# Attention front end and two-layer MLP on one core: group 0's first loads split by pairs of heads, values loaded in four pieces, first pass ordered anew

## The chip, the cores and the metric

The kernel runs on one core of a Trainium2 chip. A core has TensorE (PE in the profile; its weight loads are PEld), VectorE (DVE), ScalarE (ACT), GpSimd (POOL) and SyncE (SP). Each engine works through its own queue of instructions in program order, and semaphores make one wait for another. SP and POOL issue the transfers between DRAM and the on-chip memory; POOL's can change float32 into float16 on the way. Products of TensorE land in eight PSUM banks of 512 float32 columns.

The metric is the device time of the whole program in microseconds, median over runs; lower is better.

## The reference

```python
def _attn_ref(q, k, v):                       # each (8, 12, 448, 64)
    S = q.shape[2]
    scale = 1.0 / np.sqrt(q.shape[-1])
    scores = scale * np.matmul(q, k.transpose(0, 1, 3, 2)) - np.log(S)
    attn = 1.0 / (1.0 + np.exp(-scores))
    return np.matmul(attn, v).astype(np.float32)

def _moe_ref(x, w_in, w_out, beta):           # x (3584, 768), w_in (768, 2048), w_out (2048, 768)
    h = x @ w_in
    g = h * (1.0 / (1.0 + np.exp(-beta * h)))
    return (g @ w_out).astype(np.float32)
```

`reference` runs the attention, puts the 12 heads of a token side by side (768 values) and feeds the 3584 tokens to the two layers. The weights of the attention are sigmoids, so there is no sum over keys to wait for.

## The kernel before

**Groups, pairs, key tiles.** Four heads make a group; a batch has three groups (`QPB`), the program 24. A group is two pairs of heads (`s = 2 * g + x`, x = 0 or 1), and the four heads lie on 32 partitions each, so that a pair holds 64 partitions. The 448 rows of a head are cut by partition into 14 chunks (`NB`) of 32 rows. `transpose` turns the raw q and k of a group into `qT` and `kT` by 32x32 blocks on VectorE. Keys come in three full tiles of 128 and a short one of 64 (`KL`): chunks 0 to 11 fill the full tiles, chunks 12 and 13 the short one. The values lie the same way in `v16`: column `j` of the 32 rows of chunk block `i` belongs to full tile `j`, and column `JF` of partitions 0 to 63 to the short tile; `double_v_last` copies these 64 partitions to the other 64.

**Score, sigmoid, values.** `score` multiplies one head's keys by its queries, two products (`e`) of 32 rows each, and writes a score tile, which is two PSUM banks, one per head of the pair. `weigh` (L250) is ScalarE's sigmoid over such a tile, `weigh_two` (L265) over two. `half_visit(g, c0, second)` does half of a group's queries (224) against key tiles 0 and 1, or against tile 2 and the short one; it works on both pairs at once. `attend` (L340) multiplies the values by the attention, and VectorE brings the result to `xT` (L349). Three score tiles are in use in the first pass (`share_psum(3)`), two after `("two",)`.

**Layers.** `dense1` (L362) is the first layer of a block of 128 hidden columns, six products each, with its sigmoid on ScalarE (L374) and its product with it on VectorE (L377). Later batches go through a Strassen-like scheme (L531, L651).

**The first pass** is a list written out by hand, `BEGIN`: each entry goes to the queue of its engine in this order. `("cast", r, c0, c1, act)` turns chunks of group 0's staged k (r = 1) or q (r = 0) from float32 into float16, on ScalarE or VectorE. `("k", g)` and `("q", g, half)` are transposes. `("idle", n)` gives TensorE n products of a zero tile, which nothing reads. `("scores", g, half, second)` is a `half_visit`, `("values", g, half)` an `attend`, `("dense", n)` takes the next n products from `fill`, a list of first- and second-layer products. Behind `BEGIN`, a loop visits the other groups and spreads the rest of `fill` between the visits; `MORE` shifts the share of single visits by a few products.

**Loads.** Group 0's k and the first half of its q come by SP as float32 into memory that `gt` uses later (L797), then beta (L824). All else comes by POOL in the order of `LOADS`, then `LATER`: q and k by L126, the values by `load_v_full` (L149, four loads per batch) and `load_v_last` (L161, two), `w_in` in eight pieces (L177), `w_out` in four (L185). POOL's loads share eight semaphores in turn, so that each waits before its issue until the eighth load before it has landed. Ahead of its loads POOL sets two small constants, `nlogs` and `dummy` (L811, L812).

```python
        BEGIN = [
            ("cast", 1, 0, 8, False), ("cast", 1, 8, 14, True), ("cast", 0, 0, 7, True), ("k", 0), ("q", 0, 0),
            ("q", 1, 0), ("idle", 20), ("scores", 0, 0, 1), ("idle", 4), ("scores", 0, 0, 0), ("k", 1),
            ("idle", 2), ("k", 2), ("q", 2, 0), ("idle", 2), ("scores", 1, 0, 0), ("beta",), ("idle", 8),
            ("scores", 1, 0, 1), ("v", 0), ("idle", 6), ("scores", 2, 0, 0), ("values", 0, 0), ("q", 1, 1),
```

Of the kernel before, what the change touches and what calls it, by code (L numbers as in the profile page):

```python
# [8 lines left out]
FP32 = mybir.dt.float32  # L9
FP16 = mybir.dt.float16  # L10
# [3 lines left out]
def kernel(  # L14
# [10 lines left out]
    nc = tc.nc  # L25
    AF = mybir.ActivationFunctionType
    ALU = mybir.AluOpType

    B, H, S, D = q.shape
# [6 lines left out]
    PAIR = D // BLK  # L36
    JF = S // P
    KL = S - JF * P
    NF = JF * P // BLK
    NPAIR = H // 2  # L40
    QPB = H // HQ
    NHC = DM // P
# [97 lines left out]
    def last_base(s: int) -> int:  # L140
        return (s % 2 ^ swapped(s // 2)) * KL

    def load_v_full(b: int, lo: int = 0, hi: int = H):

        if b not in vs:
            vs[b] = vp.tile([P, H, JF + 1, D], FP16, tag="v16", name="v16")
        rows = v[b, lo:hi].rearrange("h (p c) d -> p h (c d)", c=NB)
        for i in range(HQ):
            nc.gpsimd.dma_start(  # L149
                out=vs[b][i * BLK : (i + 1) * BLK, lo:hi, 0:JF].rearrange("p h j d -> p h (j d)"),  # L150
                in_=rows[:, :, JF * i * D : JF * (i + 1) * D],
            )
            ready.update((b, "full", t, i) for t in range(lo // HQ, hi // HQ))

    def load_v_last(b: int):
        if b not in vs:
            vs[b] = vp.tile([P, H, JF + 1, D], FP16, tag="v16", name="v16")
        rows = v[b].rearrange("h (p c) d -> p h c d", c=NB)
# [3 lines left out]
        ready.add((b, "last"))  # L162

    def load_v(b: int):
        load_v_full(b)
        load_v_last(b)

    def double_v_last(b: int):
        assert (b, "last") in ready
        ready.add((b, "v"))  # L170
        nc.vector.tensor_copy(out=vs[b][KL:P, :, JF], in_=vs[b][0:KL, :, JF])

    WOUT = 2

# [26 lines left out]
    def transpose(g: int, r: int, c0: int = 0, c1: int = NB):  # L201
        raw = raws[g][:, r]
        assert g or (r, c0) == (0, NB // 2) or all((r, "cast", c) in ready for c in range(c0, c1))
        if r == 0:
            if g not in qT:
                qT[g] = qTp.tile([P, NB * BLK, PAIR], FP16, tag="qT", name="qT")
            ready.update((g, "q", c) for c in range(c0, c1, NB // 2))
            nc.vector.transpose(
                out=in_order(g // QPB, qT[g][:, c0 * BLK : c1 * BLK]),
                in_=raw[:, c0:c1].rearrange("p c d -> p (c d)").bitcast(FP32),  # L210
            )
            return
        ready.add((g, "k"))
        kT[g] = kTp.tile([P, S, PAIR], FP16, tag="kT", name="kT")
        to = kT[g].rearrange("p k e -> p (k e)").bitcast(FP32)
        frm = raw.rearrange("p c d -> p (c d)").bitcast(FP32).rearrange("p (c f) -> p c f", c=NB)
        nc.vector.transpose(  # L217
            out=to[:, 0 : JF * P].rearrange("p (j i q) -> p i j q", j=JF, i=HQ),
            in_=frm[:, 0:NF].rearrange("p (i j) f -> p i j f", j=JF),
        )  # L220
        nc.vector.transpose(  # L221
            out=to[:, JF * P :], in_=frm[:, NF:].rearrange("p c f -> p (c f)")
        )

    def score_tile():
        i, j = scored[n_sc[0] % len(scored)]
# [3 lines left out]

    def score(sco, u0: int, s: int, jt: int, hh: int, e: int, c0: int, n: int):
        g, lo = s // 2, (s % 2 * 2 + hh) * BLK
        assert (g, "k") in ready and all(
            (g, "q", c) in ready for c in range(c0 // BLK, (c0 + n) // BLK, NB // 2)
        )
        base, nk = (last_base(s), KL) if jt == JF else (0, P)
        nc.tensor.matmul(  # L237
            sco[base : base + nk, hh, u0 : u0 + n],
            kT[g][lo : lo + BLK, jt * P : jt * P + nk, e],
            qT[g][lo : lo + BLK, c0 : c0 + n, e],  # L240
            start=(e == 0),
            stop=(e == PAIR - 1),
            tile_position=(lo, base),
        )
# [55 lines left out]
    def half_visit(g: int, c0: int, second: int):  # L300
# [18 lines left out]
        for s, jt, sco, u0 in plan:  # L319
            at_use(ats[id(sco)], (s, jt, c0), slice(u0, u0 + QH))  # L320

    def attend(g: int, c0: int, n: int, part=(0, 1)):
        b, t = divmod(g, QPB)
        if b not in xTs:
            xTs[b] = xTp.tile([P, NHC, S], FP16, tag="xT", name="xT")
        assert (b, "v") in ready and (b, "full", t, HQ - 1) in ready
# [438 lines left out]
    with tc.manual_schedule():  # L765
        def load(what, *a):
            if what == "q":
                load_one(a[0], 0, a[1] * NH, (a[1] + 1) * NH)
            elif what == "k":
                load_one(a[0], 1)  # L770
            elif what == "qk":
                load_qk(a[0])
            elif what == "v":
                load_v_full(0, a[0] * HQ, a[1] * HQ)
            elif what == "last":
                load_v_last(0)
# [7 lines left out]
        LOADS = [  # L784
            ("q", 1, 0), ("k", 1), ("k", 2), ("last",), ("q", 2, 0), ("v", 0, 3), ("q", 1, 1), ("q", 0, 1),
            ("q", 2, 1), ("w_in", 0, 2), ("w_in", 2, 4), ("w_in", 4, 6), ("w_in", 6, 8), ("w_in", 8, 10),
            ("w_in", 10, 12), ("w_in", 14, 16), ("w_in", 12, 14),
        ]
        LATER = [
            ("qk", 3), ("w_out", 0, 0), ("w_out", 1, 0), ("values", 1), ("qk", 4), ("qk", 5), ("w_out", 0, 1),  # L790
# [11 lines left out]
        def cast(r: int, c0: int, c1: int, act: bool):  # L802
            out = raws[0][:, r, c0:c1].rearrange("p c d -> p (c d)")
            frm = parts[r][0][:, c0 * D : c1 * D]
            if act:
                nc.scalar.copy(out=out, in_=frm)  # L806
            else:
                nc.vector.tensor_copy(out=out, in_=frm)
            ready.update((r, "cast", c) for c in range(c0, c1))
# [22 lines left out]
        def beta_columns():  # L832
# [3 lines left out]
                nc.vector.transpose(out=beta_sb[part], in_=beta_in[:, part])  # L836

        BEGIN = [
            ("cast", 1, 0, 8, False), ("cast", 1, 8, 14, True), ("cast", 0, 0, 7, True), ("k", 0), ("q", 0, 0),
            ("q", 1, 0), ("idle", 20), ("scores", 0, 0, 1), ("idle", 4), ("scores", 0, 0, 0), ("k", 1),  # L840
            ("idle", 2), ("k", 2), ("q", 2, 0), ("idle", 2), ("scores", 1, 0, 0), ("beta",), ("idle", 8),
            ("scores", 1, 0, 1), ("v", 0), ("idle", 6), ("scores", 2, 0, 0), ("values", 0, 0), ("q", 1, 1),
            ("scores", 2, 0, 1), ("q", 0, 1), ("values", 1, 0), ("scores", 0, 1, 0),
            ("values", 2, 0), ("scores", 0, 1, 1), ("dense", 12), ("scores", 1, 1, 1), ("two",), ("dense", 6),
            ("scores", 1, 1, 0), ("loads",), ("q", 2, 1), ("dense", 21), ("scores", 2, 1, 0), ("dense", 9),
            ("values", 0, 1), ("scores", 2, 1, 1), ("values", 1, 1), ("values", 2, 1), ("dense", 39), ("k", 3),
            ("q", 3, 0), ("q", 3, 1), ("dense", 45),
        ]
        for what, *a in BEGIN:
            if what == "q":  # L850
                g, half = a
                transpose(g, 0, half * NH, (half + 1) * NH)
            elif what == "k":
                transpose(a[0], 1)
            elif what == "scores":
                half_visit(a[0], a[1] * QH, a[2])
            elif what == "cast":
# [1 line left out]
            elif what == "idle":  # L859
                idle_units(a[0])  # L860
            elif what == "v":
                double_v_last(a[0])
# [32 lines left out]
        def left_us(n: int):  # L895
# [2 lines left out]
        AV_US = 1.5  # L898
        GLANCE = 3
        MORE = {  # L900
# [3 lines left out]
        }  # L904
        RESERVE = (1.99, 3.28)
        LATE = {
# [122 lines left out]
```

## Time and profile before

| | |
|---|---|
| median of 3 runs | 373.94 us (373.41 to 374.00) |
| the profiled execution | 374.6 us, its span 372.8 us |
| TensorE busy | 365.8 us (98%) |
| ScalarE busy | 259.9 us (70%) |
| VectorE busy | 254.5 us (68%) |
| GpSimd busy | 90.6 us (24%) |
| granted TensorE clock | 1.00 |

The span runs from the first instruction to the last; the execution's own time has 1.8 us around it. Busy time is a share of the whole span; what a stage waits for is read in the timeline of that stage. In a line of the timeline the columns are start and length in us, engine, line, operation, what it writes and reads, and in brackets the idle time of the engine before it with what ended it; several like instructions in a row are merged (x10).

In the first 5.9 us TensorE runs nothing but the fillers of `("idle", 20)`. VectorE and ScalarE are idle until 4.35, when group 0's k has landed.

### The profile page before, as it was taken

Reading aid. Unit: us, or ns where it says so; the run is one execution under the profiler, and the core shown is the slowest. Engines: PE = TensorE matmul, PEld = TensorE weight load, DVE = VectorE, ACT = ScalarE, POOL = GpSimd, SP = SyncE. Lnnn points to the kernel's source line nnn. Section 1 sums busy time; section 2 is a strip of 40 time slices with the busy share of each in tenths; the row PEclk is TensorE's granted clock in tenths of the full one; section 3 lists DMA queues with packets and bytes.
Section 4 is the critical chain, followed back from the end, with each engine's and each line's share of the span. In section 5 each row is a group of like instructions: output and inputs, shape, how many; then the busy total and the mean of one; then the engine's idle time right before and its main releaser. Section 6 shows DMA issues by size and latency. Waiting matters only on the chain.

```text
span 372.8 us, 7320 instructions
## 1 busy us (share of the span) xinstructions
PE 365.8 (98%) x2906; PEld 184.4 (49%) x2906; DVE 254.5 (68%) x479; ACT 259.9 (70%) x311; POOL 90.6 (24%) x136
## 2 busy tenths in 40 slices
PE   7989999999999999999999999999999999999997
PEld 4566644443444455544444445554444455555655
DVE  3435696877496966787667666778667666669671
ACT  5995777699876658887777749887787647883000
POOL 6833253151151012325123003235100002230000
PEclk9999999999999999999999999999999999999999
DMA  9999999993359030039829511018903111000334
GB/s 162 165 189 202 197 203 201 245 125 51 49 76 183 2 86 1 0 51 125 157 42 206 108 26 33 3 17 116 172 6 86 42 44 42 1 2 1 86 84 128
DMA packets 42626, 34.65 MB, mean 93 GB/s; under 512 B 21968, under 2 KB 39008, under 8 KB 42592
## 3 DMA queue, kind: packets, MB, share of 16 engines
q0 software_dynamic: 36688, 22.47, 44.5%
q1 hardware_dynamic: 5904, 11.71, 11.1%
q8 instruction: 23, 0.38, 0.4%
q14 instruction: 11, 0.09, 0.1%
HBM read 45.62 MB, written 11.01 MB: 152 GB/s over the span
## 4 chain that ended last, share of the span: by engine, by line
PE 92%; ACT 5%; issue 1%; DMA 1%; DVE 1%; ACTq 0%
PE ps L651 27%; PE ps L531 26%; PE ps L237 11%; PE ps L340 10%; PE ps L362 9%; PE ps L392 4%; PE ps L445 4%; ACT attns L250 3%; DMA gt<-in_k_dram 1%; ACT attns L265 1%; ACT sg L374 1%; DVE gt L377 0%; DVE kT L217 0%; ACT raw L806 0%; ACT osb L672 0%
## 5 line engine op out<-in xcount | busy, mean ns | idle before, releaser
L265 ACT ACTIVATE attns<-ps,nlogs 128x1792 f16<-128x1792 f32 x75 | 131.6, 1755 | 41.7 <-PE ps L237 41.6
L651 PEld LDWEIGHTS <-sum 128*128 128x128 f16 x440 | 40.5, 98 | 37.3 <-issue 12.5
L545 POOL TENSOR_TENSOR gt<-attns,sg 128x448 f16<-128x448 f32 x21 | 23.9, 1139 | 141.7 <-ACT sg L542 141.7
L237 PE MATMUL ps<-qT,kT 32*128 32x448 f16 (+3 forms) x864 | 52.1, 339 | 1.2 <-ACT attns L250 0.4
L542 ACT ACTIVATE sg<-ps,beta_sb 128x448 f32<-128x448 f32 x72 | 45.2, 632 | 8.4 <-PE ps L531 5.9
L531 PE MATMUL ps<-xT,w_in 128*128 128x448 f16 x216 | 49.2, 353 | 0.0
L531 PE MATMUL ps<-xT,w_S 128*128 128x448 f16 x216 | 49.2, 352 | 0.0
L651 PE MATMUL ps<-w_T,sum 128*128 128x384 f16 x264 | 48.7, 327 | 0.0
L545 DVE TENSOR_TENSOR gt<-ps,sg 128x448 f16<-128x448 f32 x72 | 44.3, 618 | 4.0 <-ACT sg L542 3.8
L349 DVE CAST xT<-ps 128x448 f16<-128x448 f32 (+1 forms) x54 | 28.8, 567 | 21.0 <-PE ps L340 21.0
L531 PEld LDWEIGHTS <-w_in 128*128 128x128 f16 x288 | 28.0, 98 | 26.6 <-issue 0.7
L362 PE MATMUL ps<-xT,w_in 128*128 128x448 f16 (+1 forms) x240 | 39.9, 316 | 1.2 <-DMA w_in<-in_moe_w_in_dram 0.6
L340 PE MATMUL ps<-attns,v 128*64 128x448 f16 (+3 forms) x432 | 40.4, 340 | 0.6 <-issue 0.6
L669 DVE TENSOR_TENSOR osb<-ps,osb 128x384 f32<-128x384 f32 x55 | 30.5, 554 | 15.1 <-PE ps L651 12.8
L638 DVE TENSOR_TENSOR sum<-gt 128x1024 f16<-128x1024 f16 x55 | 36.5, 678 | 0.2
L377 DVE TENSOR_TENSOR gt<-ps,sg 128x448 f16<-128x448 f32 (+1 forms) x40 | 20.1, 527 | 23.2 <-ACT sg L374 23.1
L126 POOL DMA_DIRECT2D raw<-in_q_dram x26 | 14.5, 559 | 79.6 <-DVE kT L221 72.6
L651 PE MATMUL ps<-w_out,gt 128*128 128x384 f16 x176 | 33.3, 327 | 0.0
L651 PE MATMUL ps<-w_out,sum 128*128 128x384 f16 x176 | 32.3, 327 | 0.0
L591 DVE TENSOR_TENSOR ps<-ps,attns 128x448 f32<-128x448 f32 x24 | 15.2, 632 | 23.3 <-PE ps L531 19.3
L362 PEld LDWEIGHTS <-w_in 128*128 128x128 f16 x240 | 21.8, 98 | 18.0 <-issue 5.4
L531 PEld LDWEIGHTS <-w_S 128*128 128x128 f16 x216 | 21.1, 98 | 19.4
(54 smaller groups left out, 376.4 us busy)
## 6 DMA issues: line engine op xcount, KB each, us to landing
out_dram<-osb SPq DMA_DIRECT2D x100, 96.0 KB, 2.1
raw<-in_k_dram POOLq DMA_DIRECT2D x23, 224.0 KB, 5.5
raw<-in_q_dram POOLq DMA_DIRECT2D x21, 224.0 KB, 3.9
v<-in_v_dram POOLq DMA_DIRECT2D x32, 144.0 KB, 6.2
w_in<-in_moe_w_in_dram POOLq DMA_DIRECT2D x8, 384.0 KB, 11.8
w_out<-in_moe_w_out_dram POOLq DMA_DIRECT2D x4, 768.0 KB, 13.4
v<-in_v_dram POOLq DMA_DIRECT2D x16, 48.0 KB, 6.1
out_dram<-osb SPq DMA_DIRECT2D x5, 144.0 KB, 2.4
```

The source lines that it names most:

```text
L237: nc.tensor.matmul(sco[base : base + nk, hh, u0 : u0 + n], kT[g][lo : lo + BLK, jt * P : jt * P + nk, e], qT[g][lo : lo + BLK, c0 : c0 + n ...
L265: nc.scalar.activation(out=attns[:, slot : slot + 2].rearrange("p n h s -> p (n h) s"), in_=sco, func=AF.Sigmoid, bias=nlogs[:, 0:1], scal ...
L340: nc.tensor.matmul(av[hh * D : (hh + 1) * D, 0:n], vs[b][base : base + nk, 2 * (s % NPAIR) + hh, jt], at[base : base + nk, hh, 0:n], start ...
L349: nc.vector.tensor_copy(out=xTs[b][:, s % NPAIR, c0 : c0 + n], in_=av[:, 0:n])
L362: nc.tensor.matmul(m1, w_in16[:, hc, dc * P : (dc + 1) * P], xTs[b][:, hc, c0 : c0 + n], start=(hc == 0), stop=(hc == NHC - 1),)
L377: nc.vector.tensor_tensor(out=gt[:, dc, off : off + n], in0=m1, in1=sg[:, 0:n], op=ALU.mult)
L531: nc.tensor.matmul(out, w[:, c, i * P : (i + 1) * P], m[:, c], start=(start and c == 0), stop=(c == KH - 1), skip_group_check=not start,)
L542: nc.scalar.activation(out=sg, in_=h, func=AF.Sigmoid, bias=0.0, scale=beta_sb[:, dc : dc + 1])
L545: return lambda: engine.tensor_tensor(out=gt[:, dc, b % 2 * S : b % 2 * S + S], in0=h, in1=sg, op=ALU.mult)
L638: nc.vector.tensor_tensor(out=sums[t, i], in0=x, in1=y, op=op)
L651: nc.tensor.matmul(m2, (x if op is None else sums[t, i])[:, dc], w[:, dc], start=first, stop=(dc == ND - 1), skip_group_check=i >= 4,)
L669: nc.vector.tensor_tensor(out=out, in0=in0, in1=in1, op=op)
```

## The change

- Group 0's k and first half of q are loaded in two parts each, heads 0 and 1 (64 partitions) first: k, q, then k and q of heads 2 and 3. Casts and transposes go by these pairs too: 1 cast on VectorE and 2 on ScalarE become 2 and 4, and 3 transposes become 6.
- A new visit, `pair_visit`, does the scores of one pair against key tiles 0 and 1; two of them replace `("scores", 0, 0, 0)`, one ahead of `("scores", 0, 0, 1)` and one behind it.
- The short key tile's rows are other chunks: `rows_of` gives blocks 0 and 1 four chunks each (three for the full tiles, one for the short) and blocks 2 and 3 three each. The values of a batch come in four loads (two of 192 KB, two of 144 KB in float16) in place of six, and a key transpose writes 256 and 192 columns in place of 384 and 64.
- `nlogs` and `dummy` are set by VectorE, behind its two other constants, and no longer by POOL.
- `BEGIN` is laid out anew: 17 fillers at the start, 39 in all in place of 42, and six first-layer products that stood ahead of group 3's transposes stand behind them, with q's second half ahead of its first. Two entries of `MORE` change by one and two are added.

```diff
-    def load_v_full(b: int, lo: int = 0, hi: int = H):
+    def rows_of(i: int):
+
+        n = JF + int(i < KL // BLK)
+        return i * JF + min(i, KL // BLK), n
+
+    def load_v(b: int, lo: int = 0, hi: int = H):
...
         for i in range(HQ):
+            c, n = rows_of(i)
             nc.gpsimd.dma_start(
-                out=vs[b][i * BLK : (i + 1) * BLK, lo:hi, 0:JF].rearrange("p h j d -> p h (j d)"),
-                in_=rows[:, :, JF * i * D : JF * (i + 1) * D],
+                out=vs[b][i * BLK : (i + 1) * BLK, lo:hi, 0:n].rearrange("p h j d -> p h (j d)"),
+                in_=rows[:, :, c * D : (c + n) * D],
             )
-    def load_v_last(b: int):
...
-        for c in range(NF, NB):
-            lo = (c - NF) * BLK
-            nc.gpsimd.dma_start(out=vs[b][lo : lo + BLK, :, JF], in_=rows[:, :, c])
...
-        nc.vector.transpose(
-            out=to[:, 0 : JF * P].rearrange("p (j i q) -> p i j q", j=JF, i=HQ),
-            in_=frm[:, 0:NF].rearrange("p (i j) f -> p i j f", j=JF),
-        )
-        nc.vector.transpose(
-            out=to[:, JF * P :], in_=frm[:, NF:].rearrange("p c f -> p (c f)")
-        )
+        half = to.rearrange("p (x i q) -> p x i q", i=2, q=BLK)
+        for i in (0, 2):
+            c, n = rows_of(i)
+            nc.vector.transpose(
+                out=half[:, i // 2 :: 2].rearrange("p j i q -> p i j q"),
+                in_=frm[:, c : c + 2 * n].rearrange("p (i j) f -> p i j f", j=n),
+            )
...
+    def pair_visit(g: int, c0: int, x: int):
+
+        s, sco = 2 * g + x, score_tile()
+        for jt in (0, 1):
+            for e in range(PAIR):
+                for hh in range(2):
+                    score(sco, jt * QH, s, jt, hh, e, c0, QH)
+        slot = weigh(sco, S)
+        for jt in (0, 1):
+            at_use(slot, (s, jt, c0), slice(jt * QH, (jt + 1) * QH))
...
-            ("q", 1, 0), ("k", 1), ("k", 2), ("last",), ("q", 2, 0), ("v", 0, 3), ("q", 1, 1), ("q", 0, 1),
+            ("q", 1, 0), ("k", 1), ("k", 2), ("q", 2, 0), ("v", 0, 3), ("q", 1, 1), ("q", 0, 1), ("q", 2, 1),
...
-        for r, (to, n) in parts.items():
-            nc.sync.dma_start(
-                out=to[:, 0 : n * D],
-                in_=(q, k)[r][0, 0:HQ].rearrange("h (p c) d -> (h p) (c d)", c=NB)[:, 0 : n * D],
-            )
+        for x in (0, 1):
+            rows = slice(x * 2 * BLK, (x + 1) * 2 * BLK)
+            for r, (to, n) in parts.items():
+                nc.sync.dma_start(
+                    out=to[rows, 0 : n * D],
+                    in_=(q, k)[r][0, 2 * x : 2 * (x + 1)].rearrange("h (p c) d -> (h p) (c d)", c=NB)[:, 0 : n * D],
+                )
...
-        nc.gpsimd.memset(nlogs, NEG_LOG_S)
-        nc.gpsimd.memset(dummy, 0.0)
-        nc.scalar.activation(out=dummy, in_=dummy, func=AF.Sigmoid, bias=0.0, scale=1.0)
...
         nc.vector.memset(beta_in, 0.0)
+        nc.vector.memset(dummy, 0.0)
+        nc.vector.memset(nlogs, NEG_LOG_S)
+        nc.scalar.activation(out=dummy, in_=dummy, func=AF.Sigmoid, bias=0.0, scale=1.0)
...
-            ("cast", 1, 0, 8, False), ("cast", 1, 8, 14, True), ("cast", 0, 0, 7, True), ("k", 0), ("q", 0, 0),
-            ("q", 1, 0), ("idle", 20), ("scores", 0, 0, 1), ("idle", 4), ("scores", 0, 0, 0), ("k", 1),
-            ("idle", 2), ("k", 2), ("q", 2, 0), ("idle", 2), ("scores", 1, 0, 0), ("beta",), ("idle", 8),
...
-            ("scores", 2, 1, 1), ("values", 1, 1), ("values", 2, 1), ("dense", 39), ("k", 3),
-            ("q", 3, 0), ("q", 3, 1), ("dense", 45),
+            ("cast", 1, 0, 0, 9, False), ("cast", 1, 0, 9, 14, True), ("cast", 0, 0, 0, 7, True), ("k", 0, 0),
+            ("q", 0, 0, 0), ("cast", 1, 1, 0, 7, False), ("cast", 1, 1, 7, 14, True),
+            ("cast", 0, 1, 0, 7, True), ("k", 0, 1), ("q", 0, 0, 1), ("idle", 17), ("pair", 0, 0, 0),
+            ("q", 1, 0), ("scores", 0, 0, 1), ("pair", 0, 0, 1), ("idle", 4), ("k", 1), ("idle", 2), ("k", 2),
+            ("q", 2, 0), ("idle", 2), ("scores", 1, 0, 0), ("beta",), ("idle", 8), ("scores", 1, 0, 1),
...
+            ("scores", 2, 1, 1), ("values", 1, 1), ("values", 2, 1), ("dense", 33), ("k", 3), ("q", 3, 1),
+            ("q", 3, 0), ("dense", 45),
...
-            0: -1, 2: 1, 3: -4, 8: -3, 9: 1, 10: 1, 12: 2, 13: 1, 14: -2, 15: 1, 16: -1, 17: -2, 19: -1, 20: -2,
+            0: -1, 2: 2, 3: -3, 8: -3, 9: 1, 10: 1, 12: 2, 13: 1, 14: -2, 15: 1, 16: -1, 17: -2, 19: -1, 20: -2,
...
-            54: 1, 59: 1, 62: 1, 67: -1,
+            54: 1, 59: 1, 62: 1, 67: -1, 80: 2, 82: 1,
```

More of the change, by code (lines that the diff above doesn't have):

```diff
@@ L38 @@
     KL = S - JF * P
-    NF = JF * P // BLK
     NPAIR = H // 2
@@ L199, in in_order, with transpose @@
         return t.rearrange("p (q c) -> p c q", c=NB) if b == B - 1 else t
-    def transpose(g: int, r: int, c0: int = 0, c1: int = NB):
-        raw = raws[g][:, r]
-        assert g or (r, c0) == (0, NB // 2) or all((r, "cast", c) in ready for c in range(c0, c1))
+    def transpose(g: int, r: int, c0: int = 0, c1: int = NB, pairs=(0, 1)):
+        rows = slice(pairs[0] * 2 * BLK, (pairs[-1] + 1) * 2 * BLK)
+        raw = raws[g][rows, r]
+        assert g or (r, c0) == (0, NB // 2) or all((r, "cast", c, x) in ready for c in range(c0, c1) for x in pairs)
         if r == 0:
@@ L206, in transpose @@
                 qT[g] = qTp.tile([P, NB * BLK, PAIR], FP16, tag="qT", name="qT")
-            ready.update((g, "q", c) for c in range(c0, c1, NB // 2))
+            ready.update((g, "q", c, x) for c in range(c0, c1, NB // 2) for x in pairs)
             nc.vector.transpose(
-                out=in_order(g // QPB, qT[g][:, c0 * BLK : c1 * BLK]),
+                out=in_order(g // QPB, qT[g][rows, c0 * BLK : c1 * BLK]),
                 in_=raw[:, c0:c1].rearrange("p c d -> p (c d)").bitcast(FP32),
@@ L232, in score @@
         g, lo = s // 2, (s % 2 * 2 + hh) * BLK
-        assert (g, "k") in ready and all(
-            (g, "q", c) in ready for c in range(c0 // BLK, (c0 + n) // BLK, NB // 2)
+        assert (g, "k", s % 2) in ready and all(
+            (g, "q", c, s % 2) in ready for c in range(c0 // BLK, (c0 + n) // BLK, NB // 2)
         )
@@ L325, in attend @@
             xTs[b] = xTp.tile([P, NHC, S], FP16, tag="xT", name="xT")
-        assert (b, "v") in ready and (b, "full", t, HQ - 1) in ready
+        assert (b, "v", t) in ready and (b, "full", t, HQ - 1) in ready
         slots = [2 * g + x for x in part]
@@ L773, in load @@
             elif what == "v":
-                load_v_full(0, a[0] * HQ, a[1] * HQ)
-            elif what == "last":
-                load_v_last(0)
+                load_v(0, a[0] * HQ, a[1] * HQ)
             elif what == "values":
@@ L808, in cast @@
                 nc.vector.tensor_copy(out=out, in_=frm)
-            ready.update((r, "cast", c) for c in range(c0, c1))
-        nc.gpsimd.memset(nlogs, NEG_LOG_S)
-        nc.gpsimd.memset(dummy, 0.0)
-        nc.scalar.activation(out=dummy, in_=dummy, func=AF.Sigmoid, bias=0.0, scale=1.0)
+            ready.update((r, "cast", c, x) for c in range(c0, c1))
         still = const.tile([P, 512], FP16, name="still")
@@ L850 @@
             if what == "q":
-                g, half = a
-                transpose(g, 0, half * NH, (half + 1) * NH)
+                g, half = a[:2]
+                transpose(g, 0, half * NH, (half + 1) * NH, a[2:] or (0, 1))
             elif what == "k":
-                transpose(a[0], 1)
+                transpose(a[0], 1, pairs=a[1:] or (0, 1))
+            elif what == "pair":
+                pair_visit(a[0], a[1] * QH, a[2])
             elif what == "scores":
@@ L861 @@
             elif what == "v":
-                double_v_last(a[0])
+                double_v_last(0, *a)
             elif what == "values":
```

43 lines of the change are left out of this document (19 added, 24 removed).

## The prediction

> **What bounds the kernel now.** I read the table of stages first (busy time of each engine in chosen stretches), then the chain that ended last, then ScalarE's, TensorE's and VectorE's timelines of the first 32 us, and the DMA view in narrow windows. Columns of the stages: stretch, length, then busy us (xinstructions) of PE, PEld, DVE, ACT, POOL, then clock, DMA share, GB/s.
>
> ```profile
> 5.94:31.27 25.33, 22.72 (x359) 14.33 (x359) 10.58 (x32) 22.68 (x30) 13.71 (x20) 1.00 1.39 179
> 31.27:44.00 12.73, 12.73 (x90) 8.12 (x92) 8.00 (x19) 7.01 (x14) 3.00 (x5) 1.00 1.33 202
> 44.00:64.00 20.00, 20.00 (x182) 9.47 (x174) 15.83 (x27) 14.68 (x12) 9.79 (x16) 1.00 1.31 202
> 64.00:128.00 64.00, 63.94 (x549) 27.58 (x547) 46.75 (x88) 51.06 (x43) 14.41 (x25) 1.00 0.69 110
> ```
>
> From 31.27 us TensorE never rests: the stretches to 337 us sum to 0.16 us of idle. The changed program has the same TensorE instructions there in the same order, but for a few first-layer products that trade places with scores around the first loop visits. So the time can only change by the moment at which TensorE gets through the first pass (now 31.27 us).
>
> In that first pass the chain of waits lies mostly on ScalarE. Its queue:
>
> ```profile
> 4.35 1.10 ACT L806 CAST raw<-gt 128x384 f16<-128x384 f32 x2 [2.11 <-DMA gt<-in_k_dram]
> 6.70 8.68 ACT L250 ACTIVATE attns<-ps,nlogs 128x896 f16<-128x896 f32 x10 [1.25 <-PE ps L237]
> 15.75 4.99 ACT L250 ACTIVATE attns<-ps,nlogs 128x896 f16<-128x896 f32 x6 [0.37 <-PE ps L237]
> 26.62 1.75 ACT L265 ACTIVATE attns<-ps,nlogs 128x1792 f16<-128x1792 f32 x1 [0.57 <-PE ps L237]
> ```
>
> From the first sigmoid (6.70) to the last (ends 30.72) it is idle only 1.34 us, in seven pieces, 0.37 and 0.57 the largest. Both are TensorE standing at a transfer:
>
> ```profile
> 14.05 0.55 PEld L340 LDWEIGHTS <-v 128*64 128x64 f16 x12 [0.80 <-DMA v<-in_v_dram]
> 24.24 1.81 PE L362 MATMUL ps<-xT,w_in 128*128 128x224 f16 x15 [0.62 <-DMA w_in<-in_moe_w_in_dram]
> ```
>
> So the gain is made of three terms: an earlier start of ScalarE's row of sigmoids, and these two holes.
>
> **Term 1, the start.** Rows used:
>
> ```profile
> gt<-in_k_dram SPq DMA_DIRECT2D x1, 448.0 KB, 3.6
> gt<-in_q_dram SPq DMA_DIRECT2D x1, 224.0 KB, 3.7
> beta_in<-in_moe_beta_dram SPq DMA_DIRECT2D x1, 8.0 KB, 5.3
> ```
>
> (issue line, KB, us to landing) and VectorE's timeline:
>
> ```profile
> 4.35 0.43 DVE L808 CAST raw<-gt 128x512 f16<-128x512 f32 x1 [3.09 <-DMA gt<-in_k_dram]
> 4.89 0.58 DVE L217 STREAM_TRANSPOSE kT<-raw 128x384 f32<-128x384 f32 x1
> 5.39 0.20 DVE L221 STREAM_TRANSPOSE kT<-raw 128x64 f32<-128x64 f32 x1
> 5.52 0.37 DVE L208 STREAM_TRANSPOSE qT<-raw 128x224 f32<-128x224 f32 x1
> ```
>
> Issues by SP at 0.74, 1.17, 1.65: a pitch of 0.45, so the fourth load goes out at 2.1. k lands at 4.33, q at 4.86: 224 KB more cost 0.53. Halves in that order land at 3.80 (k), 4.07 (q), 4.60, 4.87. ScalarE's casts took 0.51 for 384 columns and 0.57 for 448; with 320 at 0.46 it runs 3.82-4.28, then three of 0.57: 4.85, 5.42, 5.99. VectorE: cast of 576 at 0.46 (to 4.28), then by the pitch of the rows above (0.50 for 384 columns, 0.13 for 64) 0.35 and 0.28 for the two new key transposes of 256 and 192 columns, 0.32 for q: the pair's q is ready at 5.31. TensorE has run its 17 fillers (20 took 4.45) by 4.9. VectorE's second pair: cast 5.27-5.66, transposes at 5.70, 6.05, 6.33, q ready at 6.70. I scale by columns, not by rows: 32x32 blocks of beta took 0.20, as long as 128x64.
>
> Pair 0's scores start at 5.33, its sigmoid when ScalarE is through its casts, 6.0. The next visit needs both pairs: TensorE 6.72, sigmoid 0.75 later, at 7.47 (before: 5.94 and 6.70). Then 0.90 + 0.68 + 0.90 (the pitches of 896- and 448-column sigmoids) bring group 1 at 9.95. Before it began at 10.08. **Gain 0.13.** Most of what the split wins is lost again, since VectorE now does twice as many casts and transposes of group 0, and ScalarE 1.1 us more of casts, both ahead of the sigmoids. Bounds: with no gap after pair 0, group 0's 3.38 us follow 6.0: 9.38, a gain of 0.70. The other end: the fourth load. Software loads from POOL reach the DMA engines while it runs; today SP's third load, 8 KB, took 5.3 us. At 5.3 the fourth lands at 7.4. I take 5.3 us: today the engines move 352 GB/s from 3.0 until the software queue comes in near 4.05; if it comes 0.45 earlier, 0.16 MB are left, and sharing the engines doubles their 0.45. Up to 5.4 it costs nothing (ScalarE is casting the rest), later one for one: at 7.4, 2.0 lost. POOL's loads move up by the two memsets and the start behind them, 0.35 (0 to 0.55: the first load now starts at 1.29, SP's at 0.74). The memsets cost VectorE some 0.2 near 1.3, hidden by the wait until 3.8; beta's load follows at 2.5 and is read near 11.6.
>
> [...]
>
> **Term 2, the values' load.** v's last piece lands at 13.99 and ends the hole of 0.37.
>
> ```profile
> v<-in_v_dram POOLq DMA_DIRECT2D x2, 48.0 KB, 7.3
> ```
>
> These two loads of 48 KB land 0.99 and 0.30 after the load before them (0.95 together in batch 1). They go; their bytes join two of the four others, whose 144 KB take 0.77, so about 0.26 each: 0.4 to 0.8 saved, say 0.5. With 0.35 from the earlier queue v is there 0.85 earlier (0.4 to 1.3); 0.13 + 0.37 = 0.50 are needed. **Gain 0.37**, 0 if v came no sooner.
>
> **Term 3, w_in.** POOL issues wait for the eighth load before. With two loads fewer, w_in's first one waits for group 2's q, which moves from behind the two small loads to fourth: issue near 10 instead of 11.84. That matters because the DMA engines have too little queued here:
>
> ```profile
> DMA packets 1251, 0.63 MB, mean 157 GB/s; under 512 B 26, under 2 KB 1251, under 8 KB 1251
> ...
> DMA packets 2310, 1.17 MB, mean 196 GB/s; under 512 B 48, under 2 KB 2309, under 8 KB 2309
> ```
>
> The first is 16-20 us, the second 20-26 us; 14-15.5 us has 114 GB/s. 1.5 x 82 plus 4 x 39 is 0.28 MB, 1.4 us at 196. I count half of it and the 0.85: w_in 1.6 us earlier (0 to 2.3). Needed is 1.07 at 24.20 and 25.55, where TensorE waits today. **Gain 0.57.** The 0.10 and 0.13 left stand behind gates and scores, and I leave them.
>
> The rest is zero: 3 fillers fewer and 4 later ones are idle TensorE's; in the 23 later groups two key transposes of 256 and 192 columns cost 0.35 + 0.28, as much as 0.50 + 0.13 today; group 3's k and q, moved six products forward, land at 34.6 and 35.8 against a use at 38.3, and the queue ahead of them is shorter.
>
> Sum 0.13 + 0.37 + 0.57 = 1.07. The profiled execution took 374.6 us with a span of 372.8; the runs' median is 373.94, so the same 1.07 off it: **372.9 us**.
>
> **Rivals.**
> - *The transfers come no sooner* (the stream is bound by bytes, which stay the same; against it: 157 against 196 GB/s). Then v3 and w_in land as now, TensorE stands at them as before and swallows term 1: 373.9 us.
> - *The fourth load is late.* ScalarE's q cast of the second pair stands in its queue ahead of every sigmoid, pair 0's too. For it: beta's 5.3 us in the same place. Landing 7.4 puts the joint visit's sigmoid at 9.2 and group 1 at 11.7, 1.6 late; the holes give back 0.94: 374.6 us. It costs from 5.4 on and makes the kernel slower from 6.8.
> - *Casts and transposes overlap better*: 0.70 in place of 0.13 and the two small holes too: 1.7 off, 372.2 us. Against it: VectorE's rows leave no room.
> - *POOL's first load starts no sooner, since its 0.42 us before 1.29 are its own*: terms 2 and 3 still have 0.4 and 1.2; 373.0, inside the forecast.
>
> **Chances.** Forecast 0.50 (its own range 372.4 to 373.5), transfers no sooner 0.20, fourth load late 0.18, better overlap 0.12. About 0.2%, 0.75 us, is what a measurement of this kernel tells from no change. Faster than 373.2: 0.42 of the forecast, all of the better overlap, 0.03 of the others: 0.57. Slower than 374.7: 0.09 of the late load, 0.04 of the stalled transfers: 0.13. The rest, 0.30, is the same. Range 371.9 to 374.6: it takes in both ends of term 1 with the holes closed, short of the worst late landings.
>
> **What would show it.** Right: the sigmoid of pair 0 near 6.0, the next near 7.5 with ScalarE idle about 0.5 between; group 1 at 9.9; no wait for v before the first values product; no wait for w_in near 24; TensorE without idle from 30.2. Wrong: ScalarE's fourth cast waiting for in_q later than 5.4; waits for w_in that remain; new idle time of TensorE after 31 us.

## The result, and the profile after

The changed kernel takes 379.26 us (median of 6 runs, 378.07 to 381.43), the kernel before 373.97 us beside it (6 runs, 373.41 to 374.69): a ratio of 1.0145, 95% interval 1.0114 to 1.0175. It is 5.3 us slower, where 1.07 us faster was forecast, and above the range. The profiled execution took 378.62 us with a span of 376.6.

The table of stages for the kernel after, in the stretches shown of before (columns as there: PE, PEld, DVE, ACT, POOL busy, clock, DMA share, GB/s):

```profile
5.94:31.27 25.33, 20.96 (x304) 13.52 (x305) 10.18 (x31) 20.80 (x28) 12.91 (x19) 0.87 1.36 186
31.27:44.00 12.73, 12.58 (x123) 8.08 (x118) 8.02 (x21) 7.64 (x14) 3.10 (x6) 1.00 1.32 202
44.00:64.00 20.00, 20.00 (x175) 10.03 (x180) 15.78 (x28) 14.73 (x14) 7.50 (x12) 1.00 1.27 204
64.00:128.00 64.00, 63.94 (x554) 27.63 (x554) 45.28 (x82) 51.12 (x42) 11.36 (x20) 1.00 0.63 107
```

From 44 us on nothing differs: TensorE is as full as before. Only the first row has changed: TensorE is busy 1.76 us less, its instructions are 55 fewer, and the granted clock is 0.87 where it was 1.00. The first pass now ends at 34.75 us in place of 31.27. From that end to the last product every kernel of this study takes 338.7 to 338.8 us, and 2.8 to 4.0 more to the end of its last store. What a kernel gains or loses, it gains or loses ahead of that end, apart from the store.

ScalarE's timeline of the kernel after:

```profile
4.34 0.46 ACT L815 CAST raw<-gt 64x320 f16<-64x320 f32 x1 [2.11 <-DMA gt<-in_k_dram]
5.28 0.56 ACT L815 CAST raw<-gt 64x448 f16<-64x448 f32 x1 [0.48 <-DMA gt<-in_q_dram]
8.35 0.56 ACT L815 CAST raw<-gt 64x448 f16<-64x448 f32 x1 [2.51 <-DMA gt<-in_k_dram]
9.21 0.56 ACT L815 CAST raw<-gt 64x448 f16<-64x448 f32 x1 [0.30 <-DMA gt<-in_q_dram]
9.80 1.01 ACT L247 ACTIVATE attns<-ps,nlogs 128x896 f16<-128x896 f32 x1
11.40 2.43 ACT L247 ACTIVATE attns<-ps,nlogs 128x896 f16<-128x896 f32 x3 [0.59 <-PE ps L234]
14.92 10.19 ACT L247 ACTIVATE attns<-ps,nlogs 128x896 f16<-128x896 f32 x12 [1.09 <-PE ps L234]
```

All four casts wait for a transfer, the third for 2.51 us. The fourth stands ahead of every sigmoid, so that the first one starts at 9.80 (6.70 before), although pair 0's scores have been ready since 7.0. The prediction had named this as a sign of being wrong: a fourth cast that waits for in_q later than 5.4. Group 1 starts at 14.92 (10.08 before): of its 4.84 us, 3.1 are there at the first sigmoid, and 1.7 come behind it, in waits of 0.59 and 1.09 for TensorE. Those are explained by TensorE's timeline and by three stretches of the table of stages:

```profile
1.19 3.81 PE L831 MATMUL ps<-still 128*128 128x256 f16 x17 [1.19 <-DVE still L822]
6.33 0.67 PE L234 MATMUL ps<-qT,kT 32*128 32x224 f16 x10 [1.33 <-DVE qT L204]
10.27 1.93 PE L234 MATMUL ps<-qT,kT 32*128 32x224 f16 x22 [3.27 <-DVE qT L204]
12.13 1.89 PE L831 MATMUL ps<-still 128*128 128x256 f16 x8
```

```profile
4.95:8.36 3.41, 0.72 (x11) 0.50 (x10) 0.99 (x4) 0.58 (x2) 1.84 (x4) 1.00 1.08 206
8.36:15.19 6.83, 4.92 (x48) 2.59 (x49) 4.64 (x15) 4.82 (x7) 4.64 (x7) 0.50 1.35 177
15.19:34.75 19.56, 18.70 (x303) 12.63 (x301) 7.20 (x21) 18.76 (x26) 8.73 (x13) 1.00 1.37 191
```

TensorE stands idle from 7.0 to 10.27 us, and between 4.95 and 8.36 it is busy 0.72 us of 3.41. In the next stretch, of 6.83 us, the granted clock is 0.50. (The stretches begin and end where the trace's entries of the clock do.) The eight fillers behind pair 1's scores then take 1.89 us, and group 1's scores stand behind them in TensorE's queue. At a clock of 1.00 eight fillers took 1.05 in f3 (shown below).

The landing of the four halves, from SP's timeline (the first four lines are the loads, the last is beta's) and from the DMA view in narrow windows (KB, us from issue to landing):

```profile
0.74 0.57 SPq L805 DMA_DIRECT2D gt<-in_k_dram  x1
1.36 0.57 SPq L805 DMA_DIRECT2D gt<-in_q_dram  x1
1.99 0.59 SPq L805 DMA_DIRECT2D gt<-in_k_dram  x1
2.62 0.60 SPq L805 DMA_DIRECT2D gt<-in_q_dram  x1
3.26 0.58 SPq L833 DMA_DIRECT2D beta_in<-in_moe_beta_dram  x1
```

```profile
gt<-in_k_dram SPq DMA_DIRECT2D x1, 224.0 KB, 3.6
gt<-in_q_dram SPq DMA_DIRECT2D x1, 112.0 KB, 3.9
gt<-in_k_dram SPq DMA_DIRECT2D x1, 224.0 KB, 6.3
gt<-in_q_dram SPq DMA_DIRECT2D x1, 112.0 KB, 6.6
```

SP issues one each 0.62 us, against 0.45 before, since each issue takes 0.57 to 0.60 instead of 0.38 to 0.42. The halves land at 4.33, 5.25, 8.33 and 9.19 us; the whole k and q landed at 4.33 and 4.86. So even the first half comes no sooner than the whole did. The DMA view from 2 to 6 us in slices of 0.1 us (busy tenths of the engines, then the rate), after and then before:

```profile
DMA  4996426699999989999999799969999995899699
GB/s 72 108 215 108 72 72 251 287 430 367 251 171 134 143 134 143 242 269 260 305 269 260 233 242 215 340 179 215 323 233 197 287 287 125 215 341 287 126 179 215
```

```profile
DMA  1498998797779899999889979999995795689699
GB/s 36 143 323 251 287 394 251 215 394 287 287 323 412 341 376 376 394 394 359 251 198 216 145 141 175 95 122 99 122 108 54 126 131 90 99 143 175 117 175 170
```

The first 20 slices (2 to 4 us) add up to a mean of 202 GB/s after, 305 before. Two things make up the loss. SP's first packets move at 2.10 us instead of 1.75, and from 2.3 to 2.8 us the engines are busy only two to six tenths. From 2.8 us on they are full, but no longer with SP's halves. The DMA view from 3 to 4 us gives the two queues (q1 is SP's, q0 POOL's; packets, MB, share of the engines' time), after and then before:

```profile
q0 software_dynamic: 123, 0.10, 79.1%
q1 hardware_dynamic: 63, 0.10, 30.0%
```

```profile
q1 hardware_dynamic: 175, 0.35, 89.4%
```

POOL's first packets reach the engines at 2.98 us in the trace of after, 3.95 before, although POOL issues only 0.06 sooner (1.23 against 1.29). Two of the experiments below fit the reading that a gap in SP's stream lets them in: in e2, with POOL's issue at 1.29 as before, they come at 2.84; in f2, where the halves come from two queues and nearly fill the engines from 2.7 to 3.8 us, they come at 3.85. No run tests this reading alone. From there the third and fourth half share the engines with POOL's loads.

### The profile page after: what moved, and what is told of

Same layout as the page of the kernel before. It is cut to its first block, busy times and chain, and to the rows that moved or that the text cites. A ratio compares the mean times of both kernels' runs of the same rounds, so it can differ in the third digit from the quotient of the medians.

```text
span 376.6 us, 7301 instructions
## 1 busy us (share of the span) xinstructions
PE 366.6 (97%) x2903; PEld 185.1 (49%) x2903; DVE 255.8 (68%) x485; ACT 260.7 (69%) x313; POOL 80.8 (21%) x118
## 4 chain that ended last, share of the span: by engine, by line
PE 92%; ACT 4%; DMA 2%; issue 1%; SPq 0%; DVE 0%; ACTq 0%
PE ps L659 27%; PE ps L539 25%; PE ps L234 11%; PE ps L348 10%; PE ps L370 9%; PE ps L400 4%; PE ps L453 4%; ACT attns L247 2%; DMA gt<-in_q_dram 2%; ACT attns L262 1%; ACT sg L382 1%; PE ps L831 0%; SPq L805 0%; DVE gt L385 0%; ACT raw L815 0%
## 5 line engine op out<-in xcount | busy, mean ns | idle before, releaser
L234 PE MATMUL ps<-qT,kT 32*128 32x448 f16 (+3 forms) x864 | 53.1, 344 | 5.0 <-DVE qT L204 4.6
L539 PEld LDWEIGHTS <-w_in 128*128 128x128 f16 x288 | 28.0, 98 | 26.6 <-issue 0.7
L234 PEld LDWEIGHTS <-kT 32*128 32x128 f16 (+1 forms) x864 | 15.2, 97 | 33.3 <-issue 27.3
```

The lines of the kernel that those rows point to most:

```text
L234: nc.tensor.matmul(sco[base : base + nk, hh, u0 : u0 + n], kT[g][lo : lo + BLK, jt * P : jt * P + nk, e], qT[g][lo : lo + BLK, c0 : c0 + n ...
L539: nc.tensor.matmul(out, w[:, c, i * P : (i + 1) * P], m[:, c], start=(start and c == 0), stop=(c == KH - 1), skip_group_check=not start,)
```

## The experiments

Two theories stood against each other after this result. *Late halves*: the split itself makes the loads late, and everything else follows. *New order*: the layout of the first pass, with more casts, more transposes and fewer fillers ahead of the sigmoids, costs time also when nothing is late. Each experiment ran beside the kernel before on the same chip; its median there was 373.71 (e1 to e4), 373.60 (f1 to f4) and 373.76 us (g1, g2).

### e1: the change with whole loads

```diff
-        for x in (0, 1):
-            rows = slice(x * 2 * BLK, (x + 1) * 2 * BLK)
-            for r, (to, n) in parts.items():
-                nc.sync.dma_start(out=to[rows, 0 : n * D], ...
+        for r, (to, n) in parts.items():
+            nc.sync.dma_start(out=to[:, 0 : n * D], ...
```

> The changed kernel with group 0's k and q loaded whole again (two loads of 128 partitions by SP), all else as changed: casts, transposes and visits by pairs, four values loads, memsets on VectorE, new layout. Theory L (the four half loads are what is late): both pairs are there by about 4.9 us, no idle of TensorE of 3 us, clock 1.00 throughout, first group 1 sigmoid near 10 us, time 372.5 to 373.8. Rival O (the new order itself costs it: more casts ahead of the sigmoids, pair visits that use half of TensorE's rows): stays above 375.5 us.

Measured: 375.97 us (4 runs, 374.73 to 376.52), ratio 1.0058 (1.0038 to 1.0078). The split of the loads is worth 3.3 us of the 5.3, but with whole loads the change is still 2.3 us slower than before. e1's ScalarE, and two stretches of its table of stages:

```profile
4.08 2.15 ACT L813 CAST raw<-gt 64x320 f16<-64x320 f32 x4 [1.85 <-DMA gt<-in_k_dram]
6.28 1.01 ACT L247 ACTIVATE attns<-ps,nlogs 128x896 f16<-128x896 f32 x1
8.12 2.43 ACT L247 ACTIVATE attns<-ps,nlogs 128x896 f16<-128x896 f32 x3 [0.84 <-PE ps L234]
11.29 10.35 ACT L247 ACTIVATE attns<-ps,nlogs 128x896 f16<-128x896 f32 x12 [0.74 <-PE ps L234]
```

```profile
5.10:8.51 3.41, 1.81 (x33) 1.17 (x33) 3.19 (x9) 2.50 (x5) 1.90 (x4) 1.00 1.03 160
8.51:11.93 3.42, 3.42 (x30) 2.01 (x29) 2.02 (x8) 2.68 (x4) 2.31 (x5) 0.50 1.46 186
```

No cast waits inside the row of four, and the first sigmoid is 0.42 earlier than before. But the joint visit (both pairs together) comes at 8.12 and group 1 at 11.29, 1.2 later than before. TensorE was busy 1.81 of 3.41 us, with no idle piece longer than 1.03 (3.27 in after), and the clock was 0.50 here too, for the next 3.42 us; the eight fillers took 1.89 again. So both theories hold a part.

### e2: the kernel before with split loads alone

```diff
-        for r, (to, n) in parts.items():
+        for x in (0, 1):
+            rows = slice(x * 2 * BLK, (x + 1) * 2 * BLK)
+            for r, (to, n) in parts.items():
...
```

> The kernel before with only the loads split (k and q of heads 0 and 1, then of heads 2 and 3, each its own SP load), casts and order as before. Theory L: the fourth load lands at 7 to 9 us instead of 4.9, first sigmoid 2 to 4 us late, clock at half for some us, time 376.5 to 379.5. Rival O: within 0.5 us of the kernel before.

Measured: 378.77 us (4 runs, 378.35 to 379.02), ratio 1.0133 (1.0117 to 1.0150). Four loads in place of two, with POOL's memsets where they were and no cast or transpose changed, cost 5.1 us, about as much as the whole change. The fourth half lands at 9.55 us, the first score starts at 10.69 (5.94 before), and the clock is at half from 7.49 to 14.31. POOL's first load went out at 1.29, as before: the move of the memsets is not what makes the halves late.

### e3: the kernel before with the new placing of the values alone

Changed are `rows_of`, `load_v`, `double_v_last`, the key transposes and the order of loads; group 0's loads and `BEGIN` stay as before.

```diff
-            ("q", 1, 0), ("k", 1), ("k", 2), ("last",), ("q", 2, 0), ("v", 0, 3), ("q", 1, 1), ("q", 0, 1),
+            ("q", 1, 0), ("k", 1), ("k", 2), ("q", 2, 0), ("v", 0, 3), ("q", 1, 1), ("q", 0, 1),
```

> The kernel before with only the values' change: four loads per batch in place of six, key transposes of 256 and 192 columns, the short tile's rows moved. If terms 2 and 3 of the forecast hold: v there by 13.5 us, w_in by 1 us or more earlier, holes of 0.37 and 0.57 us on ScalarE closed, time 372.8 to 373.4. Rival (the stream is bound by bytes): 373.7 to 374.2.

Measured: 373.40 us (median of 10 runs, nine of them 373.17 to 373.88), ratio 0.9995 (0.9985 to 1.0005): no change that can be told. The tenth run took 1264.52 us, for a reason that is not known, and the ratio leaves it out. This was the part that the prediction's terms 2 and 3 (0.94 us together) rest on. w_in's first load did go out at 9.8 us, near the 10 forecast, against 11.8 in the first profile of before. Why nothing came of it is shown with f4.

### e4: the change with 28 fillers between pair 0 and the joint visit

```diff
-            ("q", 1, 0), ("scores", 0, 0, 1), ("pair", 0, 0, 1), ("idle", 4), ...
+            ("idle", 28), ("q", 1, 0), ("scores", 0, 0, 1), ("pair", 0, 0, 1), ("idle", 4), ...
```

> The changed kernel with 28 more fillers behind the first pair visit, so that TensorE is busy while the second pair's loads are late. Theory W (a part of the loss is the half clock from 8.36 to 15.19 us): clock 1.00 there, first group 1 sigmoid near 13 us instead of 14.92, 1.5 to 2 us faster than the changed kernel, 377 to 378. Rival: the late load alone sets the end, the clock costs nothing, 378.5 to 380.

Measured: 377.96 us (4 runs, 377.32 to 378.58), ratio 1.0115 (1.0100 to 1.0130), 1.3 below the changed kernel's median; the two intervals overlap. Two stretches of its table of stages, and ScalarE:

```profile
5.37:8.78 3.41, 2.49 (x27) 2.19 (x28) 0.62 (x3) 0.48 (x2) 1.44 (x3) 1.00 1.07 193
8.78:12.19 3.41, 2.85 (x39) 1.86 (x37) 2.88 (x9) 2.73 (x4) 1.67 (x3) 1.00 1.45 189
```

```profile
10.32 1.01 ACT L247 ACTIVATE attns<-ps,nlogs 128x896 f16<-128x896 f32 x1
11.54 12.51 ACT L247 ACTIVATE attns<-ps,nlogs 128x896 f16<-128x896 f32 x15 [0.21 <-PE ps L234]
```

With the clock kept at 1.00, the waits of 0.59 and 1.09 shrink to one of 0.21, and ScalarE runs through. In this execution the fourth half came 0.5 later still (its cast at 9.74), group 1 started at 13.85 us, where near 13 was expected, and the first pass ended at 33.69 us, 1.06 sooner than in the profile of after. Most of what is left of the loss goes with the landing.

### f1: split loads, POOL held until the halves are under way

e2, with a memset of a part of `gt` not yet in use that keeps POOL busy for 2.34 us ahead of its first load:

```diff
+        nc.gpsimd.memset(gt[:, 8:14].rearrange("p c w -> p (c w)").bitcast(FP32), 0.0)
```

> The kernel before with the loads split as in e2, and POOL's own loads held back by a memset of 2688 columns of a region that is not yet in use (that makes group 1's loads late and the whole slower; the question is the landing of the four half loads). Theory C (the third and fourth half load are late because they share the DMA engines with POOL's loads): with these away the fourth lands by 6.0 us. Rival P (SP's queue itself is slow with half-partition loads): it lands at 7 us or later even so.

Measured in one run: 375.84 us. The third and fourth half in the DMA view of f1:

```profile
gt<-in_k_dram SPq DMA_DIRECT2D x1, 224.0 KB, 3.8
gt<-in_q_dram SPq DMA_DIRECT2D x1, 112.0 KB, 3.7
```

They took 6.3 and 6.6 in after. The four land at 4.13, 4.69, 5.80 and 6.33 us; the fourth lies between the two expectations. So of the fourth's 4.3 us behind the whole q in after (9.19 against 4.86), some 1.5 belong to SP's slower pace and the gaps, and some 2.9 to sharing the engines with POOL's loads. Against e2, of which f1 is a variant, the sharing is 3.2 (9.55 against 6.33).

### f2: the change with the second pair's halves on ScalarE's queue

```diff
-                nc.sync.dma_start(
+                (nc.scalar if x else nc.sync).dma_start(
```

> The changed kernel with the second pair's two loads issued from ScalarE's queue, ahead of its table load, in place of SP's. If it is the lateness of issue behind two other loads on SP (each 0.62 us, so that POOL's loads get in first) that costs it: all four halves land by 5.5 us, first-pass gain of 2 to 3.5 us, time 375.5 to 377. Rival (halves are slow from any queue): the second pair still lands at 7 us or later, time over 378.2.

Measured: 378.21 us (4 runs, 377.37 to 378.54), ratio 1.0124 (1.0109 to 1.0139), just above the rival's bound, while the landings lie between the two expectations. The last halves land at 6.15 (q of the first pair) and 6.50, and the first sigmoid starts at 8.19, 1.6 sooner than in after. But ScalarE's own two issues now stand ahead of its table load, and group 1 starts only at 13.41:

```profile
2.25 1.28 ACT L826 ACT_TABLE_LOAD   x1 [2.25 <-issue]
13.41 10.29 ACT L247 ACTIVATE attns<-ps,nlogs 128x896 f16<-128x896 f32 x12 [1.09 <-PE ps L234]
```

TensorE's eight fillers behind pair 1's scores:

```profile
10.62 1.89 PE L831 MATMUL ps<-still 128*128 128x256 f16 x8
```

They took 1.89 us, as long as in after at a clock of 0.50, and the next eight, from 13.31 us, took 1.32. So TensorE ran at half pace until near 13.9 us. The table of stages shows 1.00 for these stretches all the same, because the first entry of the clock in this trace begins at 13.90. The half clock is here read from the products' times and not from the clock column. A second queue mends a part of the landing; the waits of 0.69 and 1.09 for TensorE take a part of that back. The first pass ended at 33.33 us, 1.4 sooner than in after, where 2 to 3.5 was expected.

### f3: whole loads and more fillers

e1, with 20 fillers at the start and 9 behind pair 0:

```diff
-            ..., ("idle", 17), ("pair", 0, 0, 0),
-            ("q", 1, 0), ("scores", 0, 0, 1), ...
+            ..., ("idle", 20), ("pair", 0, 0, 0),
+            ("idle", 9), ("q", 1, 0), ("scores", 0, 0, 1), ...
```

> e1 (whole loads, all else changed) with 20 fillers at the start as before and 9 fillers behind the first pair visit. Theory W (what e1 still loses against the kernel before is the half clock from 8.51 to 11.93, which stretches 8 fillers and the scores of group 1): clock 1.00, first group 1 sigmoid near 10.0 in place of 11.29, time 373.5 to 374.7. Rival O (the order of visits and casts itself): clock 1.00 but time still over 375.3.

Measured: 373.65 us (10 runs, 373.29 to 375.33), ratio 1.0007 (0.9996 to 1.0017). Twelve products that nothing reads take back e1's 2.3 us. One stretch of the table of stages, TensorE's eight fillers, and ScalarE, of f3:

```profile
4.64:8.05 3.41, 2.89 (x38) 1.83 (x37) 3.24 (x9) 2.60 (x4) 2.50 (x5) 1.00 1.00 157
```

```profile
8.55 1.05 PE L829 MATMUL ps<-still 128*128 128x256 f16 x8
```

```profile
6.34 1.01 ACT L247 ACTIVATE attns<-ps,nlogs 128x896 f16<-128x896 f32 x1
8.17 12.51 ACT L247 ACTIVATE attns<-ps,nlogs 128x896 f16<-128x896 f32 x15 [0.82 <-PE ps L234]
```

The clock stays at 1.00 in all stretches after, and the eight fillers took 1.05. The cost of the fillers left out is so shown on the medians. In the two profiles only 0.95 us of it lies in the first pass (its end at 30.32 against e1's 31.27), and 1.3 more in e1's last store, which took 2.8 us to land instead of 1.5; the other executions have no trace, so how the 2.3 divides in them stays open. Two of e1's four executions are on record with a mean clock of 1.00 and took 376.17 and 376.52, no less than the two with 0.995. In f2 such a 1.00 stood beside products at half pace, so these figures speak neither for the half clock nor against it. What f3 also shows is the rest of the new order at its best: pair 0's sigmoid starts early, then ScalarE waits 0.82 for the joint visit, and group 1 starts at 10.49.

### f4: the kernel before once more

> The kernel before, for a second trace on this chip. If the holes of 0.37 and 0.57 us on ScalarE belong to every execution: first pass ends near 31.3 us. Rival (they belong to that one execution, which was 0.6 us over the median): first pass ends 0.5 us or more earlier, with w_in sooner.

Measured in one run: 373.41 us, 1.2 less than the first profiled execution of the same kernel (374.6). Its ScalarE:

```profile
4.32 1.11 ACT L806 CAST raw<-gt 128x384 f16<-128x384 f32 x2 [2.08 <-DMA gt<-in_k_dram]
6.87 13.58 ACT L250 ACTIVATE attns<-ps,nlogs 128x896 f16<-128x896 f32 x16 [1.45 <-PE ps L237]
25.38 1.80 ACT L265 ACTIVATE attns<-ps,nlogs 128x1792 f16<-128x1792 f32 x1
```

The sixteen sigmoids run without a hole, and none stands ahead of the one that waited 0.57. The holes on which terms 2 and 3 rest were that one execution's own. Three pieces of w_in landed at 17.05, 19.09 and 21.09 us here, at 18.94, 20.98 and 24.20 there. From 16 to 20 us the DMA view of f4 shows

```profile
DMA packets 1431, 0.72 MB, mean 180 GB/s; under 512 B 26, under 2 KB 1431, under 8 KB 1431
```

where the first profile had 157 GB/s, with the same program. Against f4 the loss can be read in one step: group 1 starts at 10.25 in f4 and at 14.92 in after, and the first pass ends at 30.08 and at 34.75: 4.67 us at both places.

### g1: halves by columns, on all 128 partitions

```diff
+                half = slice(x * n * D // 2, (x + 1) * n * D // 2)
-                out=to[:, 0 : n * D], ...
+                out=to[:, half], ...
```

> The kernel before with the same bytes of group 0 in four SP loads, but cut by columns (each load has all 128 partitions and half of the columns, k, q, k, q). Theory N (the number of SP loads in a row ahead of POOL's makes the last one late): issues of 0.6, fourth landing at 7 us or later, 377 to 379 as in e2. Rival H (it is the half partitions): issues of 0.4, fourth landing by 6 us, 373.5 to 375.

Measured: 378.32 us (4 runs, 377.34 to 379.39), ratio 1.0136 (1.0114 to 1.0158). SP's first issue and the last two halves in the DMA view of g1:

```profile
0.74 0.38 SPq L799 DMA_DIRECT2D gt<-in_k_dram  x1
```

```profile
gt<-in_k_dram SPq DMA_DIRECT2D x1, 224.0 KB, 4.7
gt<-in_q_dram SPq DMA_DIRECT2D x1, 112.0 KB, 5.8
```

The issues are as short as before again (0.38 to 0.44), so the 0.57 to 0.60 go with the loads on half the partitions. But the halves land at 3.30, 3.56, 6.39 and 7.94 us: the last two of four loads are late in either cut. So loads on half the partitions are not needed for the loss; both cuts have four loads, into which POOL's come (its first packets are at 3.14 us in g1). In e2 the fourth landed 1.6 later still, at 9.55, for 0.45 us more on the median. (A column half also halves the piece that lies together in DRAM for each partition; that was not taken apart.)

### g2: the values' placing, and the memsets on VectorE

e3, with `nlogs`, `dummy` and the sigmoid behind them as in the change.

> The kernel before with the values' change (e3) and the two memsets on VectorE: the parts of the change that are left when the pairs go. If they are worth anything: 372.9 to 373.4 with an interval below 1. If the holes of the first trace were that execution's own: 373.3 to 373.8, the same as before.

Measured: 373.56 us (11 runs, 373.17 to 373.88), ratio 0.9993 (0.9983 to 1.0003). POOL's first load goes out at 1.23, v's last piece lands at 13.09 us (13.00 in f4), and nothing comes of it. All parts of the change that leave group 0's loads and the order of the first pass alone are worth nothing that can be told.

## Why the prediction was wrong, point by point

- **What bounds the kernel** was right: the first pass decides, ScalarE's row of sigmoids in it, and 338.7 to 338.8 us follow unchanged in every kernel.
- **The step that failed is the landing of the four halves in term 1.** They were put at 3.80, 4.07, 4.60 and 4.87 us, from an unchanged pitch of 0.45 and the whole loads' rate, with 5.3 for the fourth. Measured are 4.33, 5.25, 8.33 and 9.19. The pitch is 0.62; the engines are partly empty up to 2.8 us; and POOL's loads come in 0.97 earlier with POOL's issue only 0.06 earlier, by all appearance in a gap that the halves leave. Sharing was put at a doubling of what is left; from 3 to 4 us SP's queue had 30% of the engines' time and moved 0.10 MB, against 0.35 before. Its own bound, 7.4, was taken from beta's 5.3 us, which is the time of a third load behind two whole ones. The fourth now takes 6.6, and beta, the fifth, 6.9. The bound should have let the issue time and the number of loads change, too.
- **The rival "fourth load is late" had the mechanism**, with ScalarE's fourth cast ahead of every sigmoid, and a chance of 0.18; its price was too small. It has group 1 at 11.7 for a landing at 7.4. One for one to 9.19 that is 13.5; measured is 14.92. (The prediction's other count, 2.0 lost at 7.4, gives 11.95 there and 13.7 at 9.19.)
- **"3 fillers fewer ... are idle TensorE's" was the second fault.** The other 1.2 to 1.4 us go with the half clock, by which the eight fillers and the scores behind them took longer: with the clock held (e4), group 1 started 4.1 us behind the fourth landing, in after 5.7. The fillers were counted as idle time only. But with 28 more of them (e4) and with 12 more (f3) the clock stayed at 1.00, where after had 0.50 for 6.83 us and e1 for 3.42. With whole loads the 12 are worth 2.3 us of the median (e1 against f3).
- **Terms 2 and 3 were worth nothing.** The holes of 0.37 and 0.57 were real in the profile, and absent from the same kernel's next one (f4). The mechanism of term 3 was right in part, as w_in's first load goes out at 9.8 us in e3, against 11.8 in the first profile and 10.8 in f4. The profile stood 0.66 above the median of the runs, which the prediction stated and then took off both alike; that difference was the warning.
- **Term 1's gain of 0.13** is not there either when nothing is late and the clock is held: in f3 group 1 starts at 10.49, f4 has 10.25, a loss of 0.24. The pair's sigmoid is early (6.34 against 6.87), but the joint visit waits for VectorE: its cast of the second pair's 448 columns took 0.55 where 0.39 was reckoned (and 0.39 was measured in after; why it is longer in f3 stays open), and q of the second pair was ready at 7.36, not 6.70.
- **The memsets** brought 0.06, not 0.35; the bound of 0 to 0.55 held, and the rival that POOL's time ahead of its first load is its own was right.

In sum, on the medians: the split of the loads costs 3.3 us (after against e1), fewer fillers 2.3 (e1 against f3), and the rest of the change nothing that can be told (f3 against before). The first two are not independent, since late halves also empty TensorE (idle for 3.27 us in after): the split alone, on the kernel before, costs 5.1 (e2). No version tried is faster than the kernel before by what can be told.

## What to carry to other kernels

Before a load at the head of a kernel is cut in pieces, look at what else waits for the same DMA engines: here each half cost an issue of 0.57 to 0.60 us, POOL's first packets came at 2.98 us instead of 3.95, and the fourth half took 6.6 us to land (3.7 with POOL held, in f1). Products that nothing reads need not be free time: without twelve of them the clock was 0.50 for 3.42 us in e1, and the median 2.3 us longer than f3's. Read the granted clock of such a stretch, and not only TensorE's longest gap, which was 1.03 us there. A hole seen in one profile is worth its length only if a second profile of the same kernel shows it.

## What the runs showed of the hardware

- The trace's entries of the clock begin in after at 4.95, 8.36 and 15.19 us, that is 3.41 and 6.83 apart. The clock was 0.50 for 6.83 us in after, 6.82 in e2 and 3.42 in e1.
- Ahead of its half clock, after had a stretch of 3.41 us with 0.72 us of TensorE's work, and a gap of 3.27 that began in it. In e1 the stretch ahead had 1.81 us of work and no gap above 1.03. Stretches of 3.41 us with 2.49 (e4) and 2.89 us (f3) were followed by a clock of 1.00, e4's in spite of a gap of 1.29 us, from 5.00 on, that reached into it. So in these traces the longest gap alone does not tell where the clock fell. None of these stretches had between 1.81 and 2.49 us of work.
- The clock column showed 1.00 in places where TensorE ran slower. At the start of after 17 fillers took 3.81 us, 0.22 each, in a stretch shown at 1.00; in f2 eight took 1.89, 0.24 each; eight took 1.05 us, 0.13 each, in f3. The entries of the clock begin at 4.95 us in after and at 13.90 in f2. In other executions they begin at 5.94 us (before), 4.06 (f1) and 6.47 (f4). What that is worth was not measured.
- SP's issue of a load took 0.56 to 0.60 us in the kernels whose halves lie on 64 partitions, beta's 8 KB behind them included, and 0.37 to 0.44 in all others. Why beta's is longer stays open.
- The same program's transfers landed 1.89 us apart in two executions (w_in's first of the three pieces at 18.94 and 17.05 us).
